# Softmax weights of the first seven attention tiles transposed on TensorE; fewer mask operations; new planner ranks

## The chip, the cores and the metric

The kernel runs on one core of a Trainium2 chip. The metric is device microseconds of one execution, as a median over runs. Engines: PE is TensorE (PEld its weight loads), DVE is VectorE, ACT is ScalarE, POOL is GpSimd, SP is SyncE, which here only issues DMAs. Two things lie between engines: SBUF, and PSUM, where TensorE writes and from which only DVE and ACT read in this kernel.

## The reference, cut to what matters

Attention with a local and a global window and a bias by distance (2 batches, 8 heads, 768 positions, head size 64), then a dense layer (512 to 2048 to 512, with a leaky rectifier), then a layer of 8 experts with one expert for each token.

```python
keep = is_global | is_local            # column < n_global (8), or 0 <= row - column < n_local (96)
dist = np.where(is_global & ~is_local, n_local, abs(rel))
scores = scale * q @ k.T - slope[h] * dist;  scores = where(keep, scores, -1e9)
a = exp(scores - max) ; a = a / sum(a) ; x = a @ v
h = x @ w_in ; g = max(h, 0) + alpha * min(h, 0) ; y = g @ w_out
e = argmax(y @ w_gate + modality_bias) ; out = gate * (max(y @ w1[e], 0) @ w2[e])
```

## The kernel before, in words

Tokens are handled in 12 tiles of 128 (six for each batch). Every float32 product is made of three products of a high and a low part, so most operands exist twice ("hi" and "lo").

Attention of one tile `ti` has these parts (lines 503 to 683). `attn_T` turns k and q on TensorE and splits them into hi and lo (`ring` holds k of two tiles, `qT` holds q). `attn_S` makes the scores of one half of the heads (four heads, `hh` is 0 or 1) in two PSUM banks. `attn_P` takes these banks: for each head DVE adds the bias and keeps the smallest value (`sp`, `mn`), ACT applies the exponential in place, so `sp` holds the softmax weights with the queries on partitions. The product with v needs them with the keys on partitions. So ACT writes a float16 hi part `ph`, DVE the lo part `pl`, and SP issues one DMA transpose for each into `pth`. `ph` and `pl` have one buffer, `pth` and `sp` have two. `attn_PV` multiplies `pth` with v and divides by the sum. `attn_X` turns the result and splits it into `xT`. The first tile of a batch (tiles 0 and 6) sees one block of 128 keys, the others two. `attn_V` splits v on POOL. For the first tiles of a batch the 32 global columns are kept in `kglob` and copied into `ring` by DVE from the third tile of a batch on.

The dense layer's steps (`step_a`, `step_b`) of the first weight group and the first five pairs of tiles are mixed into the attention stage: 20 steps a and 18 steps b. Their weights arrive by DMA (`load_w`) and are decoded on ACT, DVE and POOL (`decode`).

All of that is recorded and not issued at once. A planner (class `Plan`, lines 44 to 272) simulates five engines with costs written out by hand (`cost`, `AFTER`, `ISSUE`, `TURN`, `FIRST`, `DONE`) and picks on each engine, among the operations that could start within a slack, the one of the lowest rank. A rank is `slope * base + offset` with the two numbers of its kind in `URGENCY`; `SLACK` holds the slack and the time by which SP may run ahead of the DMA queue. The resulting order is fixed in each engine's instruction stream. A buffer of a rotating tag is given out in the order of the program text, whatever the order of issue: the four PSUM banks of tag `"a"` serve, for each tile, k and q of `attn_T` (2), the scores (4), `attn_PV` (2) and `attn_X` (1).

The plan is issued after the attention stage (`plan.issue(rank, *SLACK[0])`), followed by `wide_path`: every engine loads a flag and branches. The body of that branch, `dense_attention` and a repeat of the dense steps, is for windows larger than the tiles allow and doesn't run with these inputs. Then come the rest of the dense layer (a second plan) and the layer of experts, written in a fixed order.

The masks are built once, at the start: `dm0` and `bias0` for a tile that sees one block, `dm` and `bias` for the others; `sel` blends with three DVE operations.

Of the kernel before, what the change touches and what calls it, by code (L numbers as in the profile page):

```python
# [10 lines left out]
F32 = mybir.dt.float32  # L11
F32R = mybir.dt.float32r
F16 = mybir.dt.float16
# [18 lines left out]
URGENCY = {  # L32
# [6 lines left out]
}  # L39
SLACK = ((65.71, 1994.0), (185.8, math.inf))  # L40


class Plan:
# [9 lines left out]
    }  # L53
    ISSUE, TURN, FIRST, DONE = 450, 1000, 850, 1100

# [48 lines left out]
    def cost(code, name, kw, out, ins):  # L104
# [6 lines left out]
        if code == "P":  # L111
            rhs = kw.get("rhs")
            if name == "transpose":
                return 108.0, False
            if rhs.dtype == F32:
                return (226.0 if n <= 128 else n * 1.7), False
            if rhs.dtype == F32R:
                return (105.0 if rhs.ap[0][1] == 64 else 119.5 if n == 256 else 233.5 if n == 512 else max(107.0, 6 + 0.445 * n)), False
            return max(29.0, 0.43 * n + 3), False
        if code == "A":  # L120
            extra = sum(93 for k in ("bias", "scale") if aps(kw.get(k))) + (93 if "accum_out" in kw else 0)
            return (51 if psum else 92) + 0.833 * n + extra, False
        if code == "D":
# [10 lines left out]
            return 62 + (1.043 if psum else 0.522) * n + ptr + (10 if psum else 0), not psum  # L134
        if code == "G":
            return ((150 + 2.1 * n) if two else (40 + 1.1 * n)), bool(ins)
        if name == "dma_start_transpose":
            return 0.8525 * n, False
        src = kw["in_"]
        return 0.75 * (min(1800.0, max(100.0, 2.9 * n)) if src.dtype in (F32, U32) else 300.0), False  # L140

    def add(self, code, name, method, a, kw):
# [12 lines left out]
        if code == "P" and self.joined and self.ops and self.ops[-1]["code"] == "P":  # L155
            o = self.ops[-1]
            o["calls"].append(call)
            o["ns"] += cost
            o["rd"] += rd
            o["wr"] += wr  # L160
            o["tiles"].update(tiles)
        else:
            self.ops.append(
                dict(code=code, calls=[call], ns=cost, port=port, rd=rd, wr=wr, tiles=tiles, kind=self.kind, turn=name == "dma_start_transpose")
            )
# [28 lines left out]
    def simulate(self, rank, slack, ahead):  # L194
# [26 lines left out]
        while count < n:  # L221
# [23 lines left out]
            start[k] = t0  # L245
            if c == "S":
                t1 = t0 + (self.TURN if o["turn"] else self.ISSUE)
                queue = max(queue, t1 + self.FIRST) + o["ns"]
                done[k] = queue + self.DONE
                eng[c] = max(t1, queue - ahead)  # L250
            else:
# [5 lines left out]
            for t in o["tiles"]:  # L257
                users[t] -= 1
                end_of[t] = max(end_of.get(t, 0.0), done[k])
                if not users[t]:  # L260
                    free[o["tiles"][t][0], self.turn[t]] = end_of[t] + (0 if c == "S" else 150)
            for j in succ[k]:
                left[j] -= 1
                est[j] = max(est[j], done[k] + self.AFTER[c][ops[j]["code"]])
                if not left[j]:
                    ready[ops[j]["code"]].add(j)
# [15 lines left out]
def tile_kernel(  # L282
# [20 lines left out]
    GF = 4  # L303
    BT = 2
    NBK = NTT // BT
    XW = DM + 4
# [120 lines left out]


    iscr = ap1.tile([P, 2, P], I32, tag="ph", name="iscr")
    fscr = ap1.tile([P, 8, P], F32, tag="sp", name="fscr", bufs=2)  # L430
    ri, ci = iscr[:, 0], iscr[:, 1]
    rel, m1, m2, m3, dm0 = (fscr[:, j] for j in range(5))
    dm = fscr[:, 5:8]
    G.iota(ri, pattern=[[-1, P]], base=0, channel_multiplier=1)
    V.tensor_copy(out=rel, in_=ri)
    G.iota(ci, pattern=[[1, P]], base=0, channel_multiplier=0)
    colf = const.tile([P, P], F32, name="colf")
    V.tensor_copy(out=colf, in_=ci)

    def sel(o, mask, val):

        V.tensor_tensor(out=o, in0=val, in1=mask, op=ALU.mult)
        V.tensor_scalar(out=mask, in0=mask, scalar1=-BIG, scalar2=BIG, op0=ALU.mult, op1=ALU.add)
        V.tensor_tensor(out=o, in0=o, in1=mask, op=ALU.add)


    V.tensor_scalar(out=m1, in0=rel, scalar1=nl, scalar2=None, op0=ALU.is_lt)
    V.scalar_tensor_tensor(out=m1, in0=rel, scalar=0.0, in1=m1, op0=ALU.is_ge, op1=ALU.mult)  # L450

    V.tensor_scalar(out=m2, in0=colf, scalar1=ng, scalar2=None, op0=ALU.is_lt)
    V.tensor_tensor(out=m3, in0=m1, in1=m2, op=ALU.max)
    V.tensor_tensor(out=m2, in0=rel, in1=m1, op=ALU.mult)
    V.tensor_scalar(out=dm0, in0=m1, scalar1=-1.0, scalar2=1.0, op0=ALU.mult, op1=ALU.add)
    V.scalar_tensor_tensor(out=dm0, in0=dm0, scalar=nl, in1=m2, op0=ALU.mult, op1=ALU.add)
    sel(dm0, m3, dm0)
    bias0 = ap1.tile([P, H, P], BF16, name="bias0")
    bias = ap1.tile([P, H, 3, P], BF16, name="bias")
    for h in range(H):  # L460
        V.tensor_scalar(out=bias0[:, h], in0=dm0, scalar1=2.0 ** -(8.0 * (h + 1) / H), scalar2=None, op0=ALU.mult)
    with kind(0.6, "C1"):
        sel(dm[:, 1], m1, rel)

        V.tensor_scalar(out=m2, in0=rel, scalar1=float(P), scalar2=None, op0=ALU.add)
        V.tensor_scalar(out=m1, in0=m2, scalar1=nl, scalar2=None, op0=ALU.is_lt)
        V.tensor_scalar(out=m1[:, 0:NGF], in0=colf[:, 0:NGF], scalar1=ng, scalar2=None, op0=ALU.is_lt)
        V.tensor_scalar(out=m2[:, 0:NGF], in0=colf[:, 0:NGF], scalar1=0.0, scalar2=nl, op0=ALU.mult, op1=ALU.add)
        sel(dm[:, 0], m1, m2)
        V.tensor_copy(out=dm[:, 2], in_=dm[:, 0])  # L470
        for h in range(H):
            S.activation(out=bias[:, h], in_=dm, func=ACTF.Copy, scale=2.0 ** -(8.0 * (h + 1) / H))

    with kind(3.0, "C3"):
        upper = const.tile([P, P], BF16, name="upper")
        V.tensor_scalar(out=upper, in0=rel, scalar1=0.0, scalar2=None, op0=ALU.is_lt)
        ones = const.tile([P, P], BF16, name="ones")
        V.memset(ones, 1.0)
        tok1 = const.tile([P, NTT], F32, name="tok1")
# [4 lines left out]
    V.memset(cum[:, 0], 0.0)  # L484

    alpha_sb = mbs = wg = thr = None

    def more_constants():
        nonlocal alpha_sb, mbs, wg, thr
        V.memset(x2[:, :, DM:XW], 0.0)  # L490
        wg = const.tile([P, KD, 96], F32, name="wg")
        V.memset(wg, 0.0)
        Y.dma_start(out=wg[:, :, 0:E], in_=w_gate.rearrange("(k p) e -> p k e", p=P))
# [23 lines left out]
    ring = ap1.tile([P, 2, NPR, 2 * P], F32R, name="ring")  # L517
    V.memset(ring[:, :, :, P:2 * P].bitcast(F32), 0.0)
    kglob = ap1.tile([P, 2, NPR, NGF], F32R, name="kglob")
# [7 lines left out]
    def attn_T(ti):  # L527
# [19 lines left out]
        if i >= 2:  # L547
            o0 = (1 - sl) * P
            V.tensor_copy(out=ring[:, :, :, o0:o0 + NGF], in_=kglob.bitcast(F32))
        mn = sm.tile([P, H], F32, tag="mn", name="mn")  # L550
# [20 lines left out]
    def attn_P(ti, hh):  # L571
# [6 lines left out]
        for hp in range(2):  # L578
            pr = hh * 2 + hp
            c = slice(hp * 2 * P, hp * 2 * P + n)  # L580
            for r in range(2):
# [4 lines left out]
                else:  # L586
# [6 lines left out]
                    out=sp[:, h4, 0:n], in_=sp[:, h4, 0:n], func=ACTF.Exp, scale=-1.0, bias=mn[:, h:h + 1],  # L593
                )
        pth = ap1.tile([P, 2, 4 * (n // P), P], F16, tag="pth", name="pth", bufs=2)
        ph = ap1.tile([P, 4, n], F16, tag="ph", name="ph")
# [3 lines left out]
        V.scalar_tensor_tensor(out=pl, in0=sp[:, :, 0:n], scalar=PSC, in1=ph, op0=ALU.mult, op1=ALU.subtract)  # L600
        Y.dma_start_transpose(out=pth[:, 1], in_=pl.rearrange("p h c -> p (h c)"))
        z["pt"][hh] = pth

# [52 lines left out]
    def attention():  # L656

        for ti in range(NTT + 2):
            now, one, two = ti < NTT, 0 < ti <= NTT, ti > 1
            for name, on, part, t, *half in (  # L660
                ("T", now, attn_T, ti),
                ("PV0", one, attn_PV, ti - 1, 0),
                ("X", two, attn_X, ti - 2),
                ("S0", now, attn_S, ti, 0),
                ("S0", now, attn_P, ti, 0),
                ("S1", now, attn_S, ti, 1),
                ("PV1", one, attn_PV, ti - 1, 1),
                ("V", now, attn_V, ti),
# [419 lines left out]
    def wide_path(done):  # L1088
        wide = nc.values_load(fli[0:1, 0:1], min_val=0, max_val=1)
        with tc.If(wide > 0):  # L1090
            dense_attention()
# [267 lines left out]
```

## Time and profile before

| | us |
|---|---|
| median of 3 runs (lowest, highest) | 620.76 (618.43, 621.14) |
| the profiled execution: its time | 621.74 |
| the profiled execution: its span | 619.6 |

| engine | busy us | share of the span |
|---|---|---|
| PE | 570.9 | 92% |
| PEld | 509.9 | 82% |
| DVE | 385.3 | 62% |
| ACT | 307.4 | 50% |
| POOL | 211.1 | 34% |

The span runs from the first to the last instruction; the 2.1 us between it and the execution's time lie outside all instructions. Shares are averages over stages: attention with dense steps fills about 0 to 174 us, the branch stands at about 174 to 178 us, the rest of the dense layer and the experts follow.

### The profile page before, as it was taken

Reading aid. Unit: us, or ns where it says so; the run is one execution under the profiler, and the core shown is the slowest. Engines: PE = TensorE matmul, PEld = TensorE weight load, DVE = VectorE, ACT = ScalarE, POOL = GpSimd, SP = SyncE. Lnnn points to the kernel's source line nnn. Section 1 sums busy time; section 2 is a strip of 40 time slices with the busy share of each in tenths; the row PEclk is TensorE's granted clock in tenths of the full one; section 3 lists DMA queues with packets and bytes.
Section 4 is the critical chain, followed back from the end, with each engine's and each line's share of the span. In section 5 each row is a group of like instructions: output and inputs, shape, how many; then the busy total and the mean of one; then the engine's idle time right before and its main releaser. Section 6 shows DMA issues by size and latency. Waiting matters only on the chain. (4 is left out here: it accounts for less than half of the span.)

```text
span 619.6 us, 13087 instructions
## 1 busy us (share of the span) xinstructions
PE 570.9 (92%) x4476; PEld 509.9 (82%) x4476; DVE 385.3 (62%) x1007; ACT 307.4 (50%) x653; POOL 211.1 (34%) x219
## 2 busy tenths in 40 slices
PE   4569698999979999999999999998989999999995
PEld 3448587888969899898998999887879999998994
DVE  7798888878646777777422334678273259982221
ACT  3766766758536455455232333354362268862231
POOL 3434547345315546546332212222111111130120
PEclk9777879999979999999999999999999999999999
DMA  9898998996512322332000000363821299941111
GB/s 184 176 191 159 208 188 177 170 183 99 111 55 87 103 85 90 100 103 69 1 1 2 35 35 35 120 204 105 279 80 36 84 313 344 366 156 37 36 58 30
DMA packets 119856, 75.82 MB, mean 122 GB/s; under 512 B 87355, under 2 KB 107863, under 8 KB 119768
## 3 DMA queue, kind: packets, MB, share of 16 engines
q1 hardware_dynamic: 117208, 67.14, 43.0%
q0 software_dynamic: 2560, 7.64, 4.1%
q8 instruction: 39, 0.64, 0.5%
q14 instruction: 49, 0.40, 0.2%
HBM read 92.88 MB, written 7.30 MB: 162 GB/s over the span
## 5 line engine op out<-in xcount | busy, mean ns | idle before, releaser
L153 PE MATMUL h<-xT,w 128*128 128x256 f32 x888 | 117.6, 288 | 2.7 <-ACT xT L153 2.0
L153 PEld LDWEIGHTS h<-xT,w 128*128 128x128 f32 x888 | 113.3, 193 | 6.1 <-ACT xT L153 2.2
L153 PE MATMUL acc<-w,g 128*128 128x512 f32 x432 | 110.1, 402 | 4.0 <-ACTq L1090 4.0
L70 PE MATMUL h<-mw,xs 128*128 128x256 f32 x720 | 98.4, 285 | 1.2 <-ACTq L1290 0.6
L153 POOL TENSOR_TENSOR g<-t,g 128x256 fp32r<-128x256 f32 x74 | 65.1, 882 | 99.7 <-ACT g L153 59.8
L70 PE MATMUL acc<-mw,ht 128*128 128x512 f32 x360 | 97.1, 406 | 2.0 <-DVEq L1290 2.0
L153 PEld LDWEIGHTS acc<-w,g 128*128 128x128 f32 x432 | 79.8, 192 | 20.1 <-ACTq L1090 4.2
L70 PEld LDWEIGHTS h<-mw,xs 128*128 128x128 f32 x720 | 91.2, 188 | 4.6 <-DVEq L1290 1.0
L70 PEld LDWEIGHTS acc<-mw,ht 128*128 128x128 f32 x360 | 63.5, 188 | 13.7 <-DVEq L1290 2.3
L70 POOL DMA_INDIRECT out<-y,sidx x15 | 18.4, 1226 | 148.1 <-DVE y L70 116.4
L153 DVE SCALAR_TENSOR_TENSOR t<-t,alpha_sb,h 128x256 f32<-128x256 f32 x74 | 35.2, 477 | 44.9 <-ACT t L153 44.8
L70 DVE TENSOR_TENSOR mw<-raw,mw 128x1024 fp32r<-128x1024 f32 x48 | 57.6, 1223 | 8.2 <-ACT mw L70 6.5
L153 POOL TENSOR_TENSOR w<-dx,w 128x512 fp32r<-128x512 f32 x32 | 43.4, 1355 | 51.3 <-ACT w L153 48.4
L70 ACT ACTIVATE hs<-h 128x256 f32<-128x256 f32 x60 | 22.9, 381 | 70.3 <-PE h L70 62.2
L70 DVE TENSOR_TENSOR ht<-a,ht 128x256 fp32r<-128x256 f32 x60 | 25.3, 421 | 47.3 <-ACT ht L70 47.1
L153 DVE SCALAR_TENSOR_TENSOR dx<-wraw,dx 128x512 uint32<-128x512 uint32 x64 | 53.7, 843 | 0.4
L70 ACT ACTIVATE mw<-raw 128x1024 fp32r<-128x1024 f32 x48 | 49.4, 1055 | 6.1 <-issue 2.3
L153 ACT ACTIVATE t<-h 128x256 f32<-128x256 f32 x74 | 28.0, 381 | 43.6 <-PE h L153 40.6
L153 ACT ACTIVATE g<-t 128x256 fp32r<-128x256 f32 x74 | 30.8, 418 | 35.7 <-DVE t L153 30.2
L153 ACT ACTIVATE sp<-sp,mn 128x256 f32<-128x256 f32 (+1 forms) x96 | 39.3, 479 | 16.0 <-DVE mn L153 16.0
L153 PE MATMUL a<-vring,pth 128*128 128x64 bf16 (+1 forms) x880 | 35.6, 202 | 8.3 <-DMA pth<-pl 6.7
L153 PEld LDWEIGHTS <-pth 128*128 128x128 f16 x880 | 31.6, 103 | 13.0 <-DMA pth<-pl 7.9
(166 smaller groups left out, 828.3 us busy)
## 6 DMA issues: line engine op xcount, KB each, us to landing
raw<-in_moe_w SPq DMA_DIRECT2D x117, 512.0 KB
wraw<-in_moe_w_in SPq DMA_DIRECT2D x16, 512.0 KB
wraw<-in_moe_w_out SPq DMA_DIRECT2D x16, 512.0 KB
xs<-x SPq DMA_DIRECT2D x12, 258.0 KB
kr<-in_k SPq DMA_DIRECT2D x12, 256.0 KB
qr<-in_q SPq DMA_DIRECT2D x12, 256.0 KB
vr<-in_v SPq DMA_DIRECT2D x12, 256.0 KB
vring<-vglob SPq DMA_DIRECT2D x8, 96.5 KB
```

Source lines behind the costliest of these rows:

```text
L70: return method(*a, **kw)
L153: call = lambda: method(*a, **kw)
```

## The change

`attn_P` stops after the exponential for tiles below `NPE = 7` and leaves `sp` for a new part. `attn_PT` turns `sp` on TensorE in float32, four 128x128 blocks to one PSUM bank of tag `"a"` (one bank for each half of the heads in tiles 0 and 6, two in tiles 1 to 5: 96 transposes in 24 banks). ACT writes the hi part from PSUM, DVE the lo part from the same bank. 28 of the 48 DMA transposes go; tiles 7 to 11 keep theirs. The two halves' `attn_PT` are recorded behind `attn_S` of half 1 and behind `attn_T` of the next tile.

The masks use a maximum and a minimum in place of blends; part of them, the zeroing and the `kglob` copies move from DVE to POOL, `bias0` moves to ACT. The first plan's ranks and slack are new, as are some of the planner's costs for DMAs. The branch of `wide_path` gets `preferred_fallthrough_block=False`, which asks that the code behind the branch, and not its body, follow the branch instruction.

```diff
 URGENCY = {
-    "A": (0.02, 460.7), "B": (4.809, 157.8), "C": (37.78, -362.9), "C1": (0.5987, -319.9),
...
+    "A": (0.02, 228.0), "B": (0.06921, 81.0), "C": (16.99, -57.0), "C1": (17.59, 5.0),
...
-SLACK = ((65.71, 1994.0), (185.8, math.inf))
+SLACK = ((63.05, 1544.0), (185.8, math.inf))
...
-    ISSUE, TURN, FIRST, DONE = 450, 1000, 850, 1100
+    ISSUE, TURN, FIRST, DONE = 500, 1230, 850, 1400
...
+        if name == "dma_start_transpose":
+            return 1.11 * n, False
...
-        if name == "dma_start_transpose":
-            return 0.8525 * n, False
...
+    NPE = 7
...
-    def sel(o, mask, val):
-
-        V.tensor_tensor(out=o, in0=val, in1=mask, op=ALU.mult)
-        V.tensor_scalar(out=mask, in0=mask, scalar1=-BIG, scalar2=BIG, op0=ALU.mult, op1=ALU.add)
-        V.tensor_tensor(out=o, in0=o, in1=mask, op=ALU.add)
...
+    G.affine_select(out=far, in_=rel, pattern=[[-1, P]], base=0, channel_multiplier=1, compare_op=ALU.is_ge, fill=BIG)
+    V.tensor_scalar(out=cut, in0=rel, scalar1=nl, scalar2=BIG, op0=ALU.is_ge, op1=ALU.mult)
+    V.tensor_tensor(out=dm[:, 1], in0=far, in1=cut, op=ALU.max)
+
+    V.tensor_scalar(out=gcl, in0=colf, scalar1=ng, scalar2=BIG, op0=ALU.is_ge, op1=ALU.mult)
+    V.tensor_scalar(out=gcl, in0=gcl, scalar1=nl, scalar2=None, op0=ALU.max)
+
+    V.tensor_tensor(out=dm0, in0=gcl, in1=dm[:, 1], op=ALU.min)
...
     for h in range(H):
-        V.tensor_scalar(out=bias0[:, h], in0=dm0, scalar1=2.0 ** -(8.0 * (h + 1) / H), scalar2=None, op0=ALU.mult)
+        S.activation(out=bias0[:, h], in_=dm0, func=ACTF.Copy, scale=2.0 ** -(8.0 * (h + 1) / H))
...
+        G.tensor_scalar(out=far, in0=rel, scalar1=1.0, scalar2=float(P), op0=ALU.mult, op1=ALU.add)
+        V.tensor_scalar(out=cut, in0=far, scalar1=nl, scalar2=BIG, op0=ALU.is_ge, op1=ALU.mult)
+        V.tensor_tensor(out=dm[:, 0], in0=far, in1=cut, op=ALU.max)
+        G.tensor_copy(out=dm[:, 0, 0:NGF], in_=gcl[:, 0:NGF])
+        G.tensor_copy(out=dm[:, 2], in_=dm[:, 0])
...
-    V.memset(ring[:, :, :, P:2 * P].bitcast(F32), 0.0)
+    G.memset(ring[:, :, :, P:2 * P].bitcast(F32), 0.0)
...
-            V.tensor_copy(out=ring[:, :, :, o0:o0 + NGF], in_=kglob.bitcast(F32))
+            G.tensor_copy(out=ring[:, :, :, o0:o0 + NGF], in_=kglob.bitcast(F32))
...
+        if ti < NPE:
+            z["sp", hh] = sp
+            return
         pth = ap1.tile([P, 2, 4 * (n // P), P], F16, tag="pth", name="pth", bufs=2)
...
+    def attn_PT(ti, hh):
+
+        z = st[ti]
+        sp = z.pop(("sp", hh))
+        nb = 1 if ti % TPB == 0 else 2
+        spf = sp[:, :, 0:nb * P]
+        pth = ap1.tile([P, 2, 4 * nb, P], F16, tag="pth", name="pth", bufs=2)
+        for g in range(nb):
+            tp = bank(ps_a, "a").rearrange("p (a c) -> p a c", a=4)
+            for u in range(4):
+                h4, blk = divmod(g * 4 + u, nb)
+                T.transpose(tp[:, u], spf[:, h4, blk * P:(blk + 1) * P], ident)
+            o = pth[:, :, 4 * g:4 * g + 4]
+            S.activation(out=o[:, 0], in_=tp, func=ACTF.Copy, scale=PSC)
+            V.scalar_tensor_tensor(out=o[:, 1], in0=tp, scalar=PSC, in1=o[:, 0], op0=ALU.mult, op1=ALU.subtract)
         z["pt"][hh] = pth
...
                 ("T", now, attn_T, ti),
+                ("S1", one and ti <= NPE, attn_PT, ti - 1, 1),
                 ("PV0", one, attn_PV, ti - 1, 0),
...
                 ("S1", now, attn_S, ti, 1),
+                ("S0", now and ti < NPE, attn_PT, ti, 0),
                 ("PV1", one, attn_PV, ti - 1, 1),
...
-        with tc.If(wide > 0):
+        with tc.If(wide > 0, preferred_fallthrough_block=False):
```

## Rows read from the trace of the kernel before

**Rows 1.** The page: the span, and busy tenths in 40 slices of 15.5 us.

```profile
span 619.6 us, 13087 instructions
PE   4569698999979999999999999998989999999995
DVE  7798888878646777777422334678273259982221
DMA  9898998996512322332000000363821299941111
```

**Rows 2.** Stretches: us, busy us (instructions) of PE, PEld, DVE, ACT, POOL; clock, DMA, GB/s.

```profile
0.00:105.00 105.00, 73.68 (x810) 62.21 (x811) 88.84 (x300) 64.89 (x132) 49.83 (x57) 0.84 0.94 184
105.00:174.30 69.30, 69.11 (x854) 60.76 (x853) 52.50 (x163) 47.49 (x100) 30.91 (x32) 1.00 0.76 135
174.30:185.00 10.70, 6.71 (x25) 5.61 (x26) 5.19 (x10) 3.95 (x8) 0.89 (x2) 0.68 0.19 56
```

**Rows 3.** Waits in 5 to 105 us: waiting engine, tile, releaser; us, times, longest.

```profile
PE a L153 <- DMA pth<-pl: 6.7, 6, 2.4
PE a L153 <- DMA kr<-in_k: 6.1, 1, 6.1
DVE pl L153 <- DMA pth<-pl: 1.8, 2, 1.6
```

**Rows 4.** Instruction groups, DVE, 5 to 105 us: count | busy us, mean ns | idle before.

```profile
L153 DVE SCALAR_TENSOR_TENSOR pl<-sp,ph 128x1024 f16<-128x1024 f32 (+1 forms) x13 | 15.3, 1180 | 7.0 <-ACT ph L153 2.6 <-ACT xT L153 2.6 <-DMA pth<-pl 1.8
L153 DVE SCALAR_TENSOR_TENSOR qT<-a,qT 128x512 fp32r<-128x512 f32 x8 | 5.5, 682 | 2.4 <-ACT qT L153 2.3
...
L153 DVE TENSOR_TENSOR fscr<-fscr 128x128 f32<-128x128 f32 x8 | 2.1, 283 | 0.0
...
L153 DVE CAST ring<-kglob 128x256 fp32r<-128x256 f32 x4 | 1.8, 450 | 0.0
...
L153 DVE TENSOR_SCALAR bias<-fscr 128x128 bf16<-128x128 f32 x8 | 1.2, 218 | 0.0
L153 DVE TENSOR_SCALAR fscr<-fscr 128x128 f32<-128x128 f32 x5 | 1.0, 218 | 0.0
```

**Rows 5.** The chain that ended last, in the layer of experts: start, us, what.

```profile
454.86 1.43 PE h L70 x12
456.29 0.22 PE a L70 x2
456.51 1.40 PE acc L70 x6
```

**Rows 6.** DMA in 165 to 172 us: packets, MB, share of 16 engines; issues.

```profile
q1 hardware_dynamic: 2115, 0.53, 40.0%
...
pth<-ph SPq DMA_TRANSPOSE x1
pth<-pl SPq DMA_TRANSPOSE x1
```

**Rows 7.** Timeline, 159 to 166 us: start, us, engine, operation, count.

```profile
159.85 0.98 PE L153 MATMUL a<-ring,qT 64*128 64x256 f32 x12
...
161.95 1.71 ACT L153 ACTIVATE sp<-sp,mn 128x256 f32<-128x256 f32 x4
...
164.04 1.04 ACT L153 ACTIVATE ph<-sp 128x1024 f16<-128x1024 f32 x1
...
165.73 0.59 ACT L153 ACTIVATE xT<-a 128x512 fp32r<-128x512 f32 x1
```

**Rows 8.** Timeline of PE behind the branch: start, us, what, idle before and releaser.

```profile
178.28 5.32 PE L153 MATMUL acc<-w,g 128*128 128x512 f32 x12 [4.00 <-ACTq L1090]
```

**Rows 9.** The branch of `wide_path` (line 1090) on PE: ns min/median/max, start.

```profile
L1090 PEldq COMPARE_BRANCH  x1: 3592/3592/3592, 173.9 to 173.9; - x1
```

**Rows 10.** The branches of `rest` (line 1323) on PE: ns min/median/max, starts.

```profile
L1323 PEldq COMPARE_BRANCH  x5: 65/82/3597, 572.8 to 614.1; - x5
```

**Rows 11.** A stretch of 15 us with a low clock, columns as in rows 2.

```profile
30.00:45.00 15.00, 10.63 (x124) 8.63 (x124) 14.96 (x42) 9.78 (x19) 4.34 (x4) 0.67 0.87 183
```

More of the change, by code (lines that the diff above doesn't have):

```diff
@@ L119, in cost @@
             return max(29.0, 0.43 * n + 3), False
+        if name == "dma_start_transpose":
+            return 1.11 * n, False
+        if name == "dma_start":
+            return 0.75 * (min(1800.0, max(100.0, 2.9 * n)) if kw["in_"].dtype in (F32, U32) else 300.0), False
         if code == "A":
@@ L134, in cost @@
             return 62 + (1.043 if psum else 0.522) * n + ptr + (10 if psum else 0), not psum
-        if code == "G":
-            return ((150 + 2.1 * n) if two else (40 + 1.1 * n)), bool(ins)
-        if name == "dma_start_transpose":
-            return 0.8525 * n, False
-        src = kw["in_"]
-        return 0.75 * (min(1800.0, max(100.0, 2.9 * n)) if src.dtype in (F32, U32) else 300.0), False
+        return ((150 + 2.1 * n) if two else (40 + 1.1 * n)), bool(ins)
     def add(self, code, name, method, a, kw):
@@ L163, in add @@
             self.ops.append(
-                dict(code=code, calls=[call], ns=cost, port=port, rd=rd, wr=wr, tiles=tiles, kind=self.kind, turn=name == "dma_start_transpose")
+                dict(code=code, calls=[call], ns=cost, port=port, rd=rd, wr=wr, tiles=tiles, kind=self.kind, dma=name.startswith("dma_start") + (name == "dma_start_transpose"))
             )
@@ L245, in simulate @@
             start[k] = t0
-            if c == "S":
-                t1 = t0 + (self.TURN if o["turn"] else self.ISSUE)
+            if o["dma"]:
+                t1 = t0 + (self.TURN if o["dma"] == 2 else self.ISSUE)
                 queue = max(queue, t1 + self.FIRST) + o["ns"]
                 done[k] = queue + self.DONE
-                eng[c] = max(t1, queue - ahead)
+                eng[c] = max(t1, queue - ahead) if c == "S" else t1
             else:
@@ L260, in simulate @@
                 if not users[t]:
-                    free[o["tiles"][t][0], self.turn[t]] = end_of[t] + (0 if c == "S" else 150)
+                    free[o["tiles"][t][0], self.turn[t]] = end_of[t] + (0 if o["dma"] else 150)
             for j in succ[k]:
                 left[j] -= 1
-                est[j] = max(est[j], done[k] + self.AFTER[c][ops[j]["code"]])
+                est[j] = max(est[j], done[k] + self.AFTER["S" if o["dma"] else c][ops[j]["code"]])
                 if not left[j]:
@@ L430, in tile_kernel @@
     fscr = ap1.tile([P, 8, P], F32, tag="sp", name="fscr", bufs=2)
-    ri, ci = iscr[:, 0], iscr[:, 1]
-    rel, m1, m2, m3, dm0 = (fscr[:, j] for j in range(5))
+    rel, far, gcl, dm0, cut = (fscr[:, j] for j in range(5))
     dm = fscr[:, 5:8]
-    G.iota(ri, pattern=[[-1, P]], base=0, channel_multiplier=1)
-    V.tensor_copy(out=rel, in_=ri)
-    G.iota(ci, pattern=[[1, P]], base=0, channel_multiplier=0)
     colf = const.tile([P, P], F32, name="colf")
-    V.tensor_copy(out=colf, in_=ci)
-    def sel(o, mask, val):
-        V.tensor_tensor(out=o, in0=val, in1=mask, op=ALU.mult)
-        V.tensor_scalar(out=mask, in0=mask, scalar1=-BIG, scalar2=BIG, op0=ALU.mult, op1=ALU.add)
-        V.tensor_tensor(out=o, in0=o, in1=mask, op=ALU.add)
[L449 to L457, printed above, removed]
+    upper = const.tile([P, P], BF16, name="upper")
+    ones = const.tile([P, P], BF16, name="ones")
+    tok1 = const.tile([P, NTT], F32, name="tok1")
+    G.iota(iscr[:, 0], pattern=[[-1, P]], base=0, channel_multiplier=1)
+    G.tensor_copy(out=rel, in_=iscr[:, 0])
+    G.iota(iscr[:, 1], pattern=[[1, P]], base=0, channel_multiplier=0)
+    G.tensor_copy(out=colf, in_=iscr[:, 1])
+    G.affine_select(out=far, in_=rel, pattern=[[-1, P]], base=0, channel_multiplier=1, compare_op=ALU.is_ge, fill=BIG)
[4 more added lines that the diff above has]
+    V.tensor_tensor(out=dm0, in0=gcl, in1=dm[:, 1], op=ALU.min)
     bias0 = ap1.tile([P, H, P], BF16, name="bias0")
@@ L460, in tile_kernel @@
     for h in range(H):
-        V.tensor_scalar(out=bias0[:, h], in0=dm0, scalar1=2.0 ** -(8.0 * (h + 1) / H), scalar2=None, op0=ALU.mult)
+        S.activation(out=bias0[:, h], in_=dm0, func=ACTF.Copy, scale=2.0 ** -(8.0 * (h + 1) / H))
     with kind(0.6, "C1"):
[L463 to L470, printed above, removed]
+        G.tensor_scalar(out=far, in0=rel, scalar1=1.0, scalar2=float(P), op0=ALU.mult, op1=ALU.add)
[3 more added lines that the diff above has]
+        G.tensor_copy(out=dm[:, 2], in_=dm[:, 0])
         for h in range(H):
@@ L474, in tile_kernel @@
     with kind(3.0, "C3"):
[L475 to L479, printed above, removed]
+        G.memset(ones, 1.0)
+        G.affine_select(out=upper, in_=ones, pattern=[[1, P]], base=0, channel_multiplier=-1, compare_op=ALU.is_gt, fill=0.0)
         V.tensor_scalar(out=tok1, in0=colf[:, 0:NTT], scalar1=float(P), scalar2=1.0, op0=ALU.mult, op1=ALU.add)
@@ L483, in tile_kernel @@
     cum = const.tile([P, NTT + 1, E], BF16, name="cum")
-    V.memset(cum[:, 0], 0.0)
+    G.memset(cum[:, 0], 0.0)
     alpha_sb = mbs = wg = thr = None
@@ L489, in more_constants @@
         nonlocal alpha_sb, mbs, wg, thr
-        V.memset(x2[:, :, DM:XW], 0.0)
+        G.memset(x2[:, :, DM:XW], 0.0)
         wg = const.tile([P, KD, 96], F32, name="wg")
-        V.memset(wg, 0.0)
+        G.memset(wg, 0.0)
         Y.dma_start(out=wg[:, :, 0:E], in_=w_gate.rearrange("(k p) e -> p k e", p=P))
@@ L601, in attn_P @@
         Y.dma_start_transpose(out=pth[:, 1], in_=pl.rearrange("p h c -> p (h c)"))
+        z["pt"][hh] = pth
+    def attn_PT(ti, hh):
[12 more added lines that the diff above has]
+            V.scalar_tensor_tensor(out=o[:, 1], in0=tp, scalar=PSC, in1=o[:, 0], op0=ALU.mult, op1=ALU.subtract)
         z["pt"][hh] = pth
```

8 rows, old and new, of the table URGENCY are left out of this document.

## The prediction

> **What bounds the kernel now.** Read the slices of the page first [rows 1]. PE is at nine tenths from the eighth slice almost to the end; before that, in the first 105 us, it is not, while DMA stands at eight or nine and DVE at seven to nine. A change to attention can only win there, or at a gap in the stretch behind. The busy times by stretch [rows 2] put numbers on it. From 0 to 105 us PE is busy for 73.68 us at a mean granted clock of 0.84, DVE for 88.84 us (85%), the DMA engines for 94%. From 105 to 174.3 us PE is busy for 69.11 of 69.30 us at clock 1.00: that stretch is PE's, and no DMA relief can shorten it. From 174.3 to 185 us PE is busy for 6.71 of 10.70 us at clock 0.68: the gap at the branch.
>
> What does PE wait for in the first stretch? The waits [rows 3] name the first load of k (6.1 us, before any work) and the lo transposes (6.7 us). DVE itself waits only 1.8 us for a transpose. So a DMA-bound look (94%) is only half the truth: DVE at 85% stands close behind, and what DMA gives back DVE can take. I split the sum into first stretch, second stretch and branch.
>
> **The change part by part.** *DMA transposes.* In 165 to 172 us two full transposes and almost nothing else run: 40.0% of 7 us [rows 6], so 1.4 us of all 16 engines each. Of the 28 that go, 20 are full and 8 half size, 24 equivalents, 33.6 us. In the first stretch that takes the DMA load from 0.94 x 105 = 98.7 to about 65 us. DMA stops being a bound there. SP also loses 28 instructions, behind which loads of k, q, v and weights were queued.
>
> *Transposes on PE.* 96 at 0.11 us (two in 0.22 at full clock [rows 5]): 10.6 us, 21 us at half clock. PE's own work in the first stretch is at most busy time by clock, 73.68 x 0.84 = 62 us; with the new work 72.5 us. A shorter stretch still holds that.
>
> *Taking the result from PSUM.* ACT's hi part was 1.04 us for 1024 columns and becomes two of 0.59 us [rows 7]: +0.14 us for each full half, 10 of them. DVE's lo part took 15.3 us for 13 halves [rows 4]; as PSUM reads of 512 columns at 0.68 us (`qT`'s form) the same 13, ten full and three half size, cost 23 x 0.682 = 15.7 us: +0.4. So DVE saves nothing by the turn itself. PE now waits for the exponential before it can transpose, with dense matmuls and the next scores queued behind it on PE; ACT then waits for PE, DVE for ACT, `attn_PV` for DVE. Before, PE waited for `pth` only.
>
> *Masks and copies.* DVE loses eight blend operations of 2.1 us in all, eight `bias0` products of 1.2 and five scalings of 1.0 [rows 4]; its remaining mask operations are about as many as the new version's seven. That is 4.3 us at the start, where DVE is on the path to the first scores. The four `kglob` copies in this stretch take another 1.8 us off [rows 4]. POOL takes these and the zeroing over: it is busy for only 49.83 of 105 us [rows 2], so I cost them at nothing; if they delayed the split of v, by their DVE time at most 1.8 us. `bias0` on ACT, eight small operations, I cost at nothing too, since ACT is busy for 64.89 of 105 us; uncovered it costs at most what eight 256-wide exponentials do, 2 x 1.71 = 3.4 us [rows 7], and at least the 1.2 us that DVE took.
>
> *First stretch, sum.* DVE: 88.84 + 0.4 - 4.3 - 1.8 = 83.1 us of work. Its idle time is 105 - 88.84 = 16.2 us, of which 7.0 stand before the lo parts [rows 4], where it waited for ACT's hi part, for a transpose and for `xT`. I let 6 us go, since those come out of the chain that had the DMA in it: 83 + 10 = 93 us, **-12 us**. The ends: if a new wait replaces each old one, idle grows back and only about -5 is left; if DVE's idle falls to 4 us, 87 us, -18. The value taken is nearer to DVE's own row than to the DMA's, because DVE is what comes next.
>
> *Second stretch.* Its work on PE is not changed, tiles 7 to 11 keep their DMA path, PE is full. I take 0. The planner's new ranks and slack have no row; they could shift dense steps into the first stretch's remaining holes (93 - 72.5 - 6 = 14 us, of which half is a lot: -7) or leave holes here. Below, nothing excludes a loss; a granted clock that dips once as at the branch is the nearest price, +4.
>
> *The branch.* On PE the branch instruction took 3592 ns [rows 9]; of the five branches of `rest` the middle one took 82 ns and one 3597 [rows 10]. So the same instruction has two prices, 0.08 and 3.6 us, and here it is paid on the path: PE sat idle for 4.00 us [rows 8]. The dear one fits a jump over a large body, the cheap ones a fall into the code that follows; the new argument makes ours the cheap kind. That saves 3.5 us. The 12 matmuls behind the gap took 5.32 us instead of 12 x 1.40 / 6 = 2.8 [rows 5, 8], in a stretch at clock 0.68 [rows 2]; if PE no longer pauses, part of these 2.5 us goes as well. I take **-5**; the ends are 0 (the layout doesn't change, or another engine's wait stands in its place) and -6.
>
> The total is -12 + 0 - 5 = -17. Against the profiled execution, 621.74, that is 604.7; the median of the runs is 1.0 us lower (620.76), so **604 us**.
>
> **The rivals.** *A, the waits change their names.* PE's wait for the DMA becomes a wait for ACT and DVE; DVE idles as before. Then the first stretch gains no more than half of DVE's saved work, 3 us, and the branch 5: 613 us. The same time results if the attention part goes to plan but the branch stays dear (609). For it: DVE waits only 1.8 us for transposes. Against: 6.7 us of PE's waits name them.
>
> *B, nothing is left.* Added hand-overs and the new order cost what masks and branch give, 617 to 622.
>
> *C, the clock.* The new work comes in bursts of four transposes between waits, so PE pauses more often. The granted clock in the first stretch is 0.84, in 30 to 45 us 0.67 [rows 11]. If 0.67 held for the whole stretch, PE's 72.5 us would take 108 us, plus 6.1 at the start: 114 us, +9, less 5 at the branch: 625 us. It decides when PE's pauses cover the stretch as they now do in 30 to 45 us. The Trainium skill, page "TensorE: Matmul & The Clock Gate", section "A second HAM failure mode: psum-queue depth-cycling", says that PE can idle for short moments between groups of matmuls as it cycles through PSUM banks, and then swings between the two clock levels. By that rule the change would bring on this rival; before, the trace shows 1.00 in 105 to 174.3 us with the same four banks in use [rows 2], so a full PE is not hurt by them.
>
> *D, the four banks, slower.* Banks of tag "a" go round in program order. With two or four more banks for each tile, the scores of half 0 of the next tile take the banks in which half 1 of this tile was turned, so they wait until DVE has taken the lo part from there. That closes a loop for each tile: scores (two halves of 12 matmuls in 0.98), exponentials 1.71, eight transposes 0.9, two hi parts of 0.59, two lo parts of 0.68 [rows 4, 5, 7], 7.1 us, plus six hand-overs between engines. A tile now takes about 105 / 8 = 13 us. It decides when every hand-over waits for over 1 us behind other work, which DVE at 85% makes possible: at 1.5 us each the loop is 16 us, +3 for each of seven tiles, +21, less 5: 638 us. Against: unhindered, the loop has 6 us to spare.
>
> *E, more than the sum.* DVE idle falls to 4 us (-18) and dense steps fill PE's holes (half of -7), branch -6: 594 us.
>
> **How the numbers follow.** Forecast (597 to 611): 0.50. E: 0.10. A: 0.17. B: 0.09. C: 0.05. D: 0.09. The forecast, E and A are faster by over 0.5% (under 617.7), which is about what a measurement of this kernel can tell from no change: 0.77. B is within 0.5%: 0.09. C and D are slower (over 623.9): 0.14. The range has to leave out at most 0.2: D and C's end go out (0.14) and the lower part of E (0.05), so 593 to 622.
>
> **What would show it.** In the profile after: the stretch in which PE is not full ends near 93 us instead of 105; DMA there falls from 0.94 to about 0.7; DVE stands at about 90%; the wait of PE for `pth` by DMA is gone for tiles 0 to 6 and no wait of that size for ACT or DVE has come; the clock there is above 0.84; the dense layer's branch takes about 0.1 us on PE and the gap behind it is under 1 us. The prediction is wrong if the full stretch of PE begins no earlier than before (A, B), if the clock falls below 0.84 (C), if PE's waits for the lo part of half 1 before new scores add up to over 10 us (D), or if the branch still takes 3.6 us.

## The result, and the profile after

The changed kernel takes 610.22 us (median; 609.07 to 610.72) against 620.78 us for the kernel before beside it on the chip: a ratio of 0.9827, with an interval of 0.9803 to 0.9851, or 10.6 us less. The forecast was 604 us. The time lies in the range and on the side that was forecast, but 6 us above the forecast, and one of the two terms of the sum did not come at all.

The page of the changed kernel, its span and the busy tenths in 40 slices (15.2 us each), beside [rows 1]:

```profile
span 608.9 us, 13266 instructions
PE   2889999999799999999999999998999999999995
DVE  6899998686366787775222433878282269972221
DMA  7854569946134332330000000463822399940120
```

PE stands at nine from the fourth slice (46 us) on, where before it stays there from the eighth. DMA has no nine left in the first six slices; it has them in the seventh and eighth (91 to 122 us), where tiles run that keep their DMA transposes and where PE is full. The gap at the branch is still there, in the eleventh slice.

The busy times by stretch, with the columns of [rows 2] (us; busy us of PE, PEld, DVE, ACT and POOL; clock; DMA share; GB/s). First the changed kernel:

```profile
0.00:105.00 105.00, 86.76 (x1064) 76.01 (x1064) 94.56 (x322) 78.00 (x174) 58.61 (x81) 0.97 0.69 152
0.00:161.80 161.80, 142.45 (x1756) 125.43 (x1757) 131.41 (x434) 113.39 (x248) 80.77 (x108) 0.98 0.68 138
162.20:173.00 10.80, 6.91 (x24) 5.74 (x24) 5.20 (x10) 3.98 (x8) 0.90 (x2) 0.68 0.17 42
173.00:288.00 115.00, 113.96 (x723) 102.28 (x722) 82.50 (x139) 55.72 (x123) 63.39 (x62) 1.00 0.29 89
```

Then two stretches of the kernel before that were not shown: all that lies ahead of its branch, and the dense layer behind it.

```profile
0.00:173.90 173.90, 142.40 (x1660) 122.82 (x1661) 141.34 (x462) 112.03 (x230) 80.74 (x88) 0.90 0.87 165
185.00:300.00 115.00, 115.00 (x740) 104.58 (x739) 83.64 (x141) 56.82 (x126) 64.01 (x62) 1.00 0.28 88
```

The second row of the changed kernel and the first row of the kernel before tell the gain. The stretch ahead of the branch became 173.9 - 161.8 = 12.1 us shorter. PE is busy in it for the same 142.4 us, although 96 transposes were added. Its idle time fell from 173.90 - 142.40 = 31.5 us to 161.80 - 142.45 = 19.4, which is those 12.1 us. That the busy time did not grow goes with the clock: busy time by granted clock is 142.40 x 0.90 = 128.2 us before and 142.45 x 0.98 = 139.6 after, so by this estimate 11.4 us of full-speed work were added at no cost in busy time. The prediction put the transposes at 10.6 us. Counted by themselves they took more, 0.16 us each (count | busy us, mean ns | idle before; matmuls overlap, so such groups add up to more than PE's busy time):

```profile
L152 PE MATMUL a<-ident,sp 128*128 128x128 f32 x96 | 15.8, 300 | 2.0 <-DVE mn L152 1.1 <-ACT qT L152 0.5 <-DVE x L152 0.2
```

The stretch of the changed kernel in two parts, before PE is full and from there on:

```profile
0.00:46.00 46.00, 30.26 (x328) 25.90 (x330) 38.14 (x139) 30.39 (x70) 24.40 (x44) 0.93 0.73 166
46.00:161.80 115.80, 112.18 (x1430) 99.53 (x1429) 93.27 (x297) 83.00 (x179) 56.37 (x64) 1.00 0.65 127
```

The waits of PE in 5 to 105 us in the changed kernel, beside [rows 3] (waiting engine, tile, releaser; us, times, longest):

```profile
PE a L152 <- DMA kr<-in_k: 10.1, 1, 10.1
PE a L152 <- DVE pth L152: 2.2, 4, 1.2
PE a L152 <- ACT qT L152: 1.3, 2, 0.8
```

The 6.7 us for the lo transposes are gone from the top. The wait for DVE's lo part, which replaced them, costs 2.2 us. The first load of k comes 4 us later than before: more than half of the idle time that is left lies there.

Two groups of DVE's instructions in 5 to 105 us (count | busy us, mean ns | idle before), beside the first group of [rows 4]:

```profile
L152 DVE SCALAR_TENSOR_TENSOR pth<-a,pth 128x512 f16<-128x512 f32 x24 | 16.1, 686 | 1.3 <-ACT pth L152 1.1
L152 DVE SCALAR_TENSOR_TENSOR dx<-wraw,dx 128x512 uint32<-128x512 uint32 x20 | 14.3, 717 | 0.1
```

And the second of them in the kernel before, all that lie ahead of its branch (in the changed kernel these are the 20 above):

```profile
L153 DVE SCALAR_TENSOR_TENSOR dx<-wraw,dx 128x512 uint32<-128x512 uint32 x20 | 17.9, 899 | 0.0
```

The idle time ahead of the lo parts went from 7.0 to 1.3 us. The branch of the changed kernel on PE, by its source line (ns min/median/max, starts), and the timeline of PE behind it (start, us, what, idle before):

```profile
L1100 PEldq COMPARE_BRANCH  x2: 95/1866/3638, 161.8 to 162.4; - x2
```

```profile
166.10 5.49 PE L152 MATMUL acc<-w,g 128*128 128x512 f32 x12 [3.89 <-issue]
```

This answers [rows 8, 9]. There are two branch instructions now, one of 95 ns and one of 3638, PE is idle for 3.89 us instead of 4.00, and the 12 matmuls behind take 5.49 instead of 5.32. Nothing was gained here. From the first matmul behind the branch (178.28 to 166.10, 12.2 us earlier) to the end of the span (619.6 to 608.9, 10.7) some 1.5 us are lost again; about 1.0 of them shows in the dense layer's plan, where PE is busy for 113.96 of 115 us instead of all of them. These are single executions, and those of one kernel differ by more than that (618.43 to 621.14 us before).

### The profile page after: what moved, and what is told of

Read it like the earlier page. It is cut to its first block, busy times and chain, and to the rows that moved or that the text cites. A ratio compares the mean times of both kernels' runs of the same rounds, so it can differ in the third digit from the quotient of the medians.

```text
span 608.9 us, 13266 instructions
## 1 busy us (share of the span) xinstructions
PE 572.6 (94%) x4572; PEld 512.9 (84%) x4572; DVE 374.7 (62%) x979; ACT 309.1 (51%) x671; POOL 211.0 (35%) x239
## 5 line engine op out<-in xcount | busy, mean ns | idle before, releaser
L152 PE MATMUL acc<-w,g 128*128 128x512 f32 x432 | 111.1, 404 | 4.9 <-issue 3.9
L152 PE MATMUL h<-xT,w 128*128 128x256 f32 x888 | 114.7, 285 | 0.1
L152 PEld LDWEIGHTS h<-xT,w 128*128 128x128 f32 x888 | 110.8, 190 | 3.3 <-DVE t L152 0.5
L152 POOL TENSOR_TENSOR g<-t,g 128x256 fp32r<-128x256 f32 x74 | 60.2, 817 | 92.2 <-ACT g L152 62.2
L70 PEld LDWEIGHTS acc<-mw,ht 128*128 128x128 f32 x360 | 63.5, 189 | 12.2 <-DVEq L1300 0.8
L152 DVE SCALAR_TENSOR_TENSOR dx<-wraw,dx 128x512 uint32<-128x512 uint32 x64 | 50.9, 799 | 0.5
L70 POOL TENSOR_TENSOR g<-t,g 128x256 fp32r<-128x256 f32 x22 | 17.9, 815 | 58.6 <-ACT g L70 58.5
L70 PE MATMUL acc<-w,g 128*128 128x512 f32 x144 | 38.0, 400 | 0.0
```

The source lines that it names most:

```text
L70: return method(*a, **kw)
L152: call = lambda: method(*a, **kw)
```

## The experiments

Differences in us are ratios times 620.8, each kernel against the kernel before on the same chip.

### The branch

**ft_only.** The kernel before with the new argument alone:

```diff
-        with tc.If(wide > 0):
+        with tc.If(wide > 0, preferred_fallthrough_block=False):
```

> The kernel before with the new argument of the branch alone. The prediction's step (-5 us): the branch instruction on PE falls from 3.6 us to about 0.1, 616 us. The rival from the profile after, where PE shows two branch instructions (0.095 us and, right behind, 3.638 us): the cheap one falls into a short piece of code that ends with the same far jump, so nothing is gained, 621 us within 0.3%, and PE again idles for about 4 us.

Measured: 619.64 us, ratio 0.9992 [0.9976, 1.0008]. The source line of its branch on PE:

```profile
L1090 PEldq COMPARE_BRANCH  x2: 95/1726/3357, 173.9 to 174.4; - x2
```

The argument is worth nothing. With it the trace shows two branch instructions in place of one: the first takes 95 ns, as a branch that falls through, the second 3357 ns. The reading is that the compare falls through, as asked, into a second branch, which jumps over the body, and that the body is still where it was. short_body below bears this out.

**no_wide.** The changed kernel without the branch and its body, that is, without the path for larger windows:

```diff
-                    wide_path(s_i)
```

> The changed kernel without the flag, the branch and its body (the path for large windows is left out; these inputs don't take it). If the gap is the far jump: PE's idle 3.9 us and half of the slow matmuls behind it go, 604 to 606 us. If the gap is the hand-over between the two plans (weights, banks), it stays: 610 us.

Measured: 604.72 us, ratio 0.9757 [0.9737, 0.9777], which is 15.1 us below the kernel before and, by the ratios, 4.4 below the changed one (5.5 by the medians). PE's timeline at that place:

```profile
161.34 0.60 PE L152 MATMUL a<-ident,x 128*128 128x128 f32 x4
161.69 3.32 PE L152 MATMUL acc<-w,g 128*128 128x512 f32 x12
```

The gap is gone, and the 12 matmuls behind it take 3.32 instead of 5.49 us: the price of the branch is 3.89 + 2.17 = 6.1 us at its place. The 4.4 us at the end are uncertain by some 2 us (the intervals of the two ratios), so whether all of it reaches the end is not shown.

**short_body.** The changed kernel with the branch, but with a short body; the path for larger windows is left out but for one head of its attention:

```diff
-        for h in range(H):
+        for h in range(1):
...
-            for ti in range(NTT):
+            for ti in range(0):
...
-            for z in steps[:done]:
+            for z in steps[:0]:
```

> The changed kernel with a short body behind the branch: one head of the dense attention, no repeat of the dense steps (most of the path for large windows is left out; these inputs don't take it). If the price hangs on how far the taken jump goes: the second branch instruction on PE falls from 3.6 us to about 0.1 and the time to 604 to 606 us, as without the branch. If every taken jump costs this, however short: 3.6 us stay, 610 us.

Measured: 604.71 us, ratio 0.9765 [0.9738, 0.9793], the same as without a branch. Its branch on PE and the matmuls behind:

```profile
L1100 PEldq COMPARE_BRANCH  x2: 95/144/193, 161.3 to 162.7; - x2
```

```profile
163.28 3.27 PE L152 MATMUL acc<-w,g 128*128 128x512 f32 x12
```

The same two instructions now take 95 and 193 ns. So it is neither the branch nor the read of the flag that costs, but the length of the body that is jumped over. What goes on meanwhile at the long one shows in the DMA queues. In the changed kernel, from the start of the second branch to PE's next matmul (162.4 to 166.1 us), all that DMA moved are four packets of its instruction queues, 0.04 MB (packets, MB, share of 16 engines):

```profile
DMA packets 4, 0.04 MB, mean 11 GB/s; under 512 B 0, under 2 KB 0, under 8 KB 0
q14 instruction: 3, 0.02, 2.4%
q8 instruction: 1, 0.02, 2.2%
```

With the short body, in 162.2 to 166 us, there are none:

```profile
DMA packets 0, 0.00 MB, mean 0 GB/s; under 512 B 0, under 2 KB 0, under 8 KB 0
```

The Trainium skill, page "Runtime: NRT & Kernel Launch", section "Instruction fetch mechanics", says that a taken branch whose target lies outside the small window of instructions at hand has to fetch it by DMA before execution goes on. The trace agrees: 3638 ns and four packets of code over the long body, 193 ns and none over the short one. Which engine's code the packets held it does not show.

### Which part brought what ahead of the branch

Three parts act there: the turn (`attn_PT`, `NPE = 7`), the masks with what moves to POOL and ACT, and the planner's costs, ranks and slack. All pairs and single parts were run. Each edit is the part's own share of the diff shown above.

**pe_only**, the turn alone:

```diff
+    NPE = 7
...
+        if ti < NPE:
+            z["sp", hh] = sp
+            return
...
+    def attn_PT(ti, hh):
...
+                ("S1", one and ti <= NPE, attn_PT, ti - 1, 1),
...
+                ("S0", now and ti < NPE, attn_PT, ti, 0),
```

> The kernel before with the new turn on PE for tiles 0 to 6 alone; masks, ranks, planner costs and branch as before. Theory 1, the turn itself carries the gain by relieving DMA: 609 to 613 us. Theory 2, the new ranks are what lets the order use it: within 4 us of 621. Theory 3, the gain is mostly DVE's saved mask work: 617 to 620 us.

**ranks_only**, the planner alone:

```diff
-    "A": (0.02, 460.7), "B": (4.809, 157.8), "C": (37.78, -362.9), "C1": (0.5987, -319.9),
+    "A": (0.02, 228.0), "B": (0.06921, 81.0), "C": (16.99, -57.0), "C1": (17.59, 5.0),
...
-    ISSUE, TURN, FIRST, DONE = 450, 1000, 850, 1100
+    ISSUE, TURN, FIRST, DONE = 500, 1230, 850, 1400
```

> The kernel before with the new ranks, slack and planner costs alone; turns by DMA, masks as before. Theory 1 (the turn carries it): 621 us within 4, with the first load of k later by some 4 us, since weights now rank ahead of it. Theory 2 (the ranks carry it): 612 us or less. If the ranks fit only the new work: slower, 625 to 635 us.

**masks_only**, the masks, copies and zeroing alone:

```diff
-    sel(dm0, m3, dm0)
+    V.tensor_tensor(out=dm0, in0=gcl, in1=dm[:, 1], op=ALU.min)
...
-            V.tensor_copy(out=ring[:, :, :, o0:o0 + NGF], in_=kglob.bitcast(F32))
+            G.tensor_copy(out=ring[:, :, :, o0:o0 + NGF], in_=kglob.bitcast(F32))
```

> The kernel before with the new masks, copies and zeroing alone: turns by DMA, ranks, slack and planner costs of before. If DVE's saved 6 us were worth their time by themselves: 614 to 617 us. If DMA stays the bound beside it (share 0.94 in the first stretch): 619 to 621 us.

**turn_ranks**, the turn and the planner with the old masks:

```diff
...
-SLACK = ((65.71, 1994.0), (185.8, math.inf))
+SLACK = ((63.05, 1544.0), (185.8, math.inf))
...
+    NPE = 7
...
```

> Turn on PE and new ranks together, with the masks, copies and zeroing of before. Alone the turn gave -1 us and the ranks +9. If the two simply add: 628 us. If the ranks are an order that pays only with DMA freed (weights and dense steps earlier, few transposes on SP): 610 to 614 us, and the masks are then worth the rest. If the masks are what the ranks need (their time at the start): 616 to 625.

**turn_masks**, the turn and the masks with the old planner; against the changed kernel:

```diff
...
-SLACK = ((63.05, 1544.0), (185.8, math.inf))
+SLACK = ((65.71, 1994.0), (185.8, math.inf))
...
```

> Turn on PE and new masks with the ranks, slack and planner costs of before. If masks save their DVE time at the start and DVE is the bound there (the prediction's term of 4.3 + 1.8 us): 612 to 615 us. If an order fixed by the old ranks leaves the gain unused, as it did with the turn alone: 617 to 620 us.

**ranks_masks**, the changed kernel with no tile turned on PE:

```diff
-    NPE = 7
+    NPE = 0
```

> The changed kernel with all twelve tiles turned by DMA: new ranks and new masks without the turn. If the turn is what the rest needs: near the ranks alone, 624 to 629 us, so that the turn is worth 14 us or more beside the new ranks against 1 beside the old. If masks and ranks carry much without it: 612 to 618 us.

Measured:

| kernel | median us | ratio [95%] | us against before |
|---|---|---|---|
| pe_only | 618.69 | 0.9983 [0.9962, 1.0004] | -1.1 |
| ranks_only | 628.78 | 1.0132 [1.0108, 1.0157] | +8.2 |
| masks_only | 629.59 | 1.0151 [1.0117, 1.0184] | +9.4 |
| ranks_masks | 635.62 | 1.0263 [1.0246, 1.0280] | +16.3 |
| turn_masks | 615.59 | 0.9945 [0.9922, 0.9969] | -3.4 |
| turn_ranks | 613.91 | 0.9913 [0.9893, 0.9933] | -5.4 |
| all three | 610.22 | 0.9827 [0.9803, 0.9851] | -10.7 |

The stretch ahead of the branch by windows, with the columns of [rows 2], in the order of the table (its first six kernels):

```profile
0.00:170.30 170.30, 147.71 (x1743) 127.72 (x1744) 141.53 (x472) 112.57 (x240) 74.54 (x87) 0.96 0.63 131
```

```profile
0.00:181.40 181.40, 142.32 (x1662) 121.81 (x1662) 141.74 (x463) 114.01 (x232) 80.52 (x89) 0.91 0.80 158
```

```profile
0.00:182.30 182.30, 144.73 (x1651) 124.57 (x1651) 134.40 (x423) 112.53 (x237) 83.85 (x107) 0.88 0.84 157
```

```profile
0.00:188.50 188.50, 146.49 (x1662) 124.04 (x1662) 138.53 (x425) 114.94 (x240) 88.12 (x109) 0.88 0.83 152
```

```profile
0.00:168.00 168.00, 143.18 (x1753) 125.45 (x1754) 136.01 (x435) 114.22 (x249) 79.73 (x107) 0.98 0.64 133
```

```profile
0.00:167.40 167.40, 144.61 (x1756) 126.30 (x1757) 138.93 (x472) 112.96 (x240) 73.70 (x88) 0.97 0.64 133
```

What the reader is to see: PE's idle time (length less PE busy) is 22.6, 39.1, 37.6, 42.0, 24.8 and 22.8 us, against 31.5 before and 19.4 with all. Wherever the turn is in, DMA falls to 0.68 or less and the clock stands at 0.96 or more; wherever it is out, DMA stays at 0.80 or more and the clock at 0.91 or less. So the turn is what frees DMA and what lifts the clock, whatever stands beside it. But in time its worth depends on the company: -1.1 alone (its interval holds no change), -5.4 - 8.2 = -13.6 beside the new ranks, -3.4 - 9.4 = -12.8 beside the new masks, -10.7 - 16.3 = -27 beside both.

The masks take DVE's work ahead of the branch from 141.34 to 134.40 us, and yet alone they make the kernel 9.4 us slower. The longest waits of PE in 0 to 160 us of masks_only say where this shows:

```profile
PE a L153 <- DMA pth<-pl: 13.3, 8, 2.6
PE a L153 <- ACT qT L153: 7.5, 3, 4.8
```

The wait for lo transposes, 6.7 us before in the same window, has doubled. Fewer DVE operations give no reason for that; another order of SP's list would. The next run tests what an order alone can cost.

### The order by itself

**issue_455.** The kernel before with one constant of its planner changed by 5 ns, so that no operation and no rank is another and only the order differs:

```diff
-    ISSUE, TURN, FIRST, DONE = 450, 1000, 850, 1100
+    ISSUE, TURN, FIRST, DONE = 455, 1000, 850, 1100
```

> The kernel before with one planner cost moved by 5 ns (what a DMA issue takes on SP: 455 for 450); the work, the ranks and the slack are those of before, but the simulated order tips over into another one. Theory 1, the ranks of before fit one order exactly, and any other order loses some 8 to 10 us (which would also account for masks alone, +9, and for the turn alone giving only 1): 626 to 631 us. Theory 2, orders near each other cost the same, and masks and ranks alone are slower for what they do themselves beside a full DMA: within 3 us of 619.

Measured: 630.28 us, ratio 1.0150 [1.0112, 1.0188], +9.3 us. The timeline of SP, first before, then issue_455 (lines from 29 to 35 us):

```profile
31.04 0.37 SPq L153 DMA_DIRECT2D qr<-in_q  x1
31.50 0.53 SPq L153 DMA_DIRECT2D vr<-in_v  x1
32.12 2.13 SPq L153 DMA_TRANSPOSE pth<-pl  x1
```

```profile
29.95 1.23 SPq L153 DMA_TRANSPOSE pth<-pl  x1
31.27 0.53 SPq L153 DMA_DIRECT2D vr<-in_v  x1
33.19 0.37 SPq L153 DMA_DIRECT2D qr<-in_q  x1
```

Up to there SP's list is the same. Then one transpose goes ahead of a load of q, the load comes 2.1 us later, and from there on the order is another. Nothing else in the kernel was touched, and it costs as much as the masks alone. The stretch ahead of its branch, and PE's wait for lo transposes in 0 to 160 us:

```profile
0.00:183.50 183.50, 143.33 (x1662) 123.80 (x1662) 145.98 (x463) 113.41 (x233) 79.03 (x89) 0.92 0.80 156
```

```profile
PE a L153 <- DMA pth<-pl: 9.7, 7, 3.0
```

PE's idle time is 40.2 us against 31.5 before, the wait 9.7 us against 6.7: the same two rows rise as in masks_only. One such step shows that an order can cost 9 us by itself. That masks_only loses its 9.4 us, and pe_only most of its gain, in this way is likely, but not shown.

**k_first.** The changed kernel issues two loads of weights ahead of the first k. Here the first k and q get a rank ahead of everything:

```diff
-            plan.kind = (ti - 1.0, "LV" if nm == "vr" else "L")
+            plan.kind = (ti - 1.0, "LV" if nm == "vr" else "L") if ti or nm == "vr" else (-2.0, "C")
```

> The changed kernel with the first loads of k and q ranked ahead of the first two weight loads. In the profile after, PE waits 10.1 us for k at the start, before 6.1. If that start is on the path of a stage in which PE is busy for 143 of 162 us: up to 4 us less, 606 to 608 us. If the dense steps then wait for their weights, or the start is made good later: 609 to 611 us.

Measured: 613.73 us, ratio 0.9913 [0.9886, 0.9940], which is 5.3 us more than the changed kernel. PE's wait for k and the stretch up to the branch:

```profile
PE a L152 <- DMA kr<-in_k: 6.3, 1, 6.3
```

```profile
0.00:164.00 164.00, 143.88 (x1758) 124.52 (x1758) 133.52 (x435) 115.46 (x251) 82.15 (x109) 0.99 0.64 136
```

The wait falls by 3.8 us, and still the branch comes at 164.0 instead of 161.8 us: PE's idle time is 20.1 us. What was gained at the start is lost again further on. So the two loads ahead of k can't be moved by themselves at a gain. The run can't say more: it too is another order, and what a new order costs by itself is not apart from it.

### How far the turn carries

**npe12.** The changed kernel with all twelve tiles turned on PE:

```diff
-    NPE = 7
+    NPE = 12
```

> The changed kernel with all twelve tiles turned on PE: 80 more transposes, 20 fewer DMA transposes. If the stretch behind 105 us is PE's (the prediction's second stretch, DMA relief worth nothing): 80 x 0.11 = 8.8 us more work on a full engine, 616 to 620 us. If DMA still bounds that stretch (share 0.64 to 1.06 there): 606 to 610 us.

Measured: 614.9 us, ratio 0.9921 [0.9897, 0.9945], 5.8 us more than with seven. Two windows of it, and all that lies ahead of its branch:

```profile
120.00:135.00 15.00, 14.82 (x207) 13.55 (x206) 12.10 (x36) 10.88 (x24) 7.58 (x10) 1.00 0.03 9
135.00:150.00 15.00, 15.00 (x223) 13.56 (x220) 11.04 (x37) 8.75 (x20) 1.48 (x2) 1.00 0.04 9
0.00:167.50 167.50, 149.63 (x1823) 133.86 (x1824) 133.49 (x445) 116.00 (x259) 78.47 (x108) 0.97 0.43 102
```

In the two windows DMA is almost empty and PE is full at full clock. Ahead of the branch PE is busy for 149.63 us instead of 142.45, 7.2 us more, and its idle time falls by 1.5 us only (19.4 to 17.9): the stretch is 5.7 us longer, which is the loss. So there transposes that leave DMA for PE cost more than they give. 80 more at the 0.11 us of [rows 5] would be 8.8 us; here, too, part of the difference can be the new order.

## Why the prediction was right, and where it was not

**The stage ahead of the branch: -12 forecast, -12.1 measured.** The signs that the prediction named for it are there, but for the place where PE gets full. DMA in the first 105 us fell from 0.94 to 0.69 (about 0.7 forecast); DVE stands at 94.56 / 105 = 90%, with 10.4 us of idle time where 10 were forecast, though over 105 us and not over the 93 that were meant; PE's wait for `pth` by DMA is gone for the turned tiles, and the wait for DVE in its place is 2.2 us; the clock rose from 0.84 to 0.97. Of the prices, that of the lo parts holds: 24 took 16.1 us at 686 ns each, against 15.7 for 23. That of the transposes was too low: 15.8 us by themselves, against 10.6.

**But the working that led there does not fit the trace.** I bounded the stretch by DVE up to 93 us. The trace after shows PE full from 46 us on (112.18 of 115.80 us), and the 12.1 us are PE's idle time. The first stretch did not end at 93 us: besides the transposes, more of attention and of the dense steps moved into it (PE is busy for 86.76 us instead of 73.68), so that the two stretches can't be told apart any more. DVE's account adds up as well, but not as it was forecast: ahead of the branch its work fell by 9.9 us and its idle time by 2.2 (32.6 to 30.4), where about 6 of each were meant. Of the work 3.6 us are in no term: the 20 operations `dx<-wraw,dx` took 717 ns instead of 899. Which engine bounds the kernel ahead of 46 us, where DVE is busy for 38.14 us and PE for 30.26, is not settled.

**The step "planner's ranks at 0" failed.** They are worth -10.7 + 3.4 = -7.3 us beside the other two parts, at the lower end of -7 to +4, -5.4 + 1.1 = -4.3 beside the turn without the masks, and +8.2 alone, outside that range. The turn and the masks, for which the -12 was meant, brought only -3.4 with the old ranks. The sum came out because one term was too large by about what the other was too small by, which is luck. Whether the old ranks *lose* 9 us on any new list of operations (then the turn and masks are worth about -12.4 and the new ranks only restore a fit), or the new ones are better in themselves, the runs bear on but do not settle: issue_455 shows a loss of that size from the order alone, and ranks_masks (+16.3, close to 8.2 + 9.4) that two such losses can add up. The term "masks and copies", -6.1, is seen as DVE work (-6.9) and as a difference of -10.7 + 5.4 = -5.3 us beside the other two, but such a difference contains an order, too.

**The step "the branch" failed: -5 forecast, 0 measured.** Its price was about right: where the body is short or absent, 3.9 and 4.4 us are saved in the whole kernel by the ratios, and 6.1 at the place. What failed is the sentence that the new argument "makes ours the cheap kind". It changes which way the compare falls, not where the body lies, and the jump over the body is what is dear. It is also the last of the signs that the prediction named against itself: the branch still takes 3.6 us. The cheap and dear branches of [rows 10] could not tell these two apart; I took the reading that fitted the argument's name. This is the case that the prediction counted with A at 609 us, "the attention part goes to plan but the branch stays dear"; it came with 610.2.

**What was left out: the end.** Of the 12.2 us at the branch 1.5 are lost behind it in the profiled executions, about 1.0 in the dense layer's plan. Why PE is less full there was not followed. With the branch this would make up the distance, 604 + 5 + 1.5 = 610.5, but 1.5 us is less than two executions of one kernel can differ by.

**The rivals C and D.** Neither came. The rule of the Trainium skill, page "TensorE: Matmul & The Clock Gate", section "A second HAM failure mode: psum-queue depth-cycling", as the prediction read it, would have brought more swings of the clock with 24 more banks; the trace disagrees here, since the mean granted clock ahead of the branch rose from 0.90 to 0.98. And the loop through the four banks didn't close: 2.2 us of waits for the lo part, not 10.

A version that keeps the path for larger windows, but with a body that is short or lies elsewhere, should come to about 605 us as short_body does. It was not tried.

## What to carry to other kernels

Where an engine is full behind a stretch and idle in it, make the account of that engine over the whole stage: its idle time is what there is to win, and work moved onto it costs less than its price where the granted clock rises with it, as here. Never cost a new order at nothing: 5 ns in a planner's constant cost 9 us here, so a part tried alone under ranks that were fitted to another list may tell the loss of fit as much as the part. And a branch is priced by the code that it jumps over, so ask of a layout hint where the body goes, not which way the compare falls.

## What the runs showed of the hardware

- A jump over a long body took 3.4 to 3.9 us on PE (3357, 3638 and, in issue_455, 3892 ns), the same jump over a short one 0.19 (193 ns). During the long one in the changed kernel the instruction queues of DMA moved four packets, 0.04 MB, during the short one none. PE then ran 12 matmuls in 5.49 us, in a stretch at a mean granted clock of 0.68, instead of 3.3.
- More work on PE cost no busy time: with 96 transposes more, busy time ahead of the branch stayed at 142.4 us, as the mean granted clock went from 0.90 to 0.98.
- One and the same DVE operation, `dx<-wraw,dx`, took 0.68 us alone, and 1.54 and 1.63 us where POOL was splitting v. The timelines of the kernel before show it, first DVE, then POOL (start, us, what):

```profile
24.95 1.54 DVE L153 SCALAR_TENSOR_TENSOR dx<-wraw,dx 128x512 uint32<-128x512 uint32 x1
...
27.17 1.63 DVE L153 SCALAR_TENSOR_TENSOR dx<-wraw,dx 128x512 uint32<-128x512 uint32 x1
...
51.92 0.68 DVE L153 SCALAR_TENSOR_TENSOR dx<-wraw,dx 128x512 uint32<-128x512 uint32 x1
```

```profile
24.82 1.12 POOL L153 TENSOR_TENSOR vr<-vr,vring 128x512 f32<-128x512 f32 x1
26.03 0.94 POOL L153 TENSOR_SCALAR vring<-vr 128x512 bf16<-128x512 f32 x1
27.05 1.20 POOL L153 TENSOR_TENSOR vring<-vr,vring 128x512 bf16<-128x512 f32 x1
```

The Trainium skill, page "SBUF — State Buffer", section "SBUF: two separate sides", has a lock for this: a DVE operation with two SBUF inputs and a POOL operation that reads SBUF exclude each other. The trace agrees: each of the two started while a POOL operation with two inputs was under way and ended 0.55 us behind the end of it (26.49 against 25.94 us, 28.80 against 28.25).
